# Moving Pool's two-input work, summing a softmax on ScalarE, sharing k and v buffers, and a new way to choose the order of an attention and expert kernel

## The chip, the core and the metric

The kernel runs on one core of a Trainium2 chip. A core has a matrix engine (TensorE, PE in the profile), a vector engine (VectorE, DVE), an activation engine (ScalarE, ACT), a general engine (GpSimd, POOL) and a queue engine (SyncE, SP), each with its own in-order list of instructions, and DMA engines that move data between the large memory (HBM) and the on-chip memory (SBUF). Matrix results land in a small accumulator memory (PSUM). The engines wait for each other by semaphores. The metric is the device time of one execution, in microseconds (us); a lower number is better.

## What is computed

Attention with two parts, then a gated feed-forward layer, all in fp32 (`B, H, S, D = 8, 8, 576, 64`, 512 model columns, 1024 hidden columns):

```python
q_d = q.reshape(B, H, Sd, factor, D).mean(axis=3)      # factor 4, Sd 144; k_d, v_d alike
out_up = np.repeat(sm_attn(q_d, k_d, v_d), factor, axis=2)
mask = np.abs(pos[:, None] - pos[None, :]) < factor     # seven neighbours
scores = np.where(mask, scale * np.matmul(q, k.transpose(0, 1, 3, 2)), -1000000000.0)
out_local = np.matmul(softmax(scores), v)
x = (out_up + out_local).transpose(0, 2, 1, 3).reshape(B * S, H * D)
return ((x @ w1) * (x @ w2) @ w3) @ w_out
```

The weights arrive as 64-bit floats.

## The kernel before

**Units and chunks.** Each of the 8 batches is cut into 3 units of 12 positions for 16 blocks and 8 heads (192 rows of x). Two units make a chunk of 384 rows, so there are 24 units and 12 chunks. `moe(c)` takes chunk c through the feed-forward layer: for each of 8 slices `f` of the hidden columns, 24 matmuls into two `pab` tiles, ScalarE's copy `a` (L870), VectorE's product `a` (L872), and a split of it into a high and a low half, `gh` (ScalarE, L877) and `gl` (VectorE, L879); then 9 matmuls of `acc` with the folded weight `wphl` = w3 @ w_out. Three matmuls, high x high, high x low and low x high, stand for one fp32 product. `o_sb` (L887) takes the result out and SP stores it.

**The opening.** The 64-bit weights are loaded raw by SP and rebuilt to fp32 on chip: ScalarE's rebase (L285) and low word (L293, or Pool's L295), VectorE's L298 and L302. `fold` multiplies w3 by w_out on TensorE (`accw`, L337), and `gate_weights` splits w1 and w2 into a high half (ScalarE, L384) and a low half (Pool's subtraction, L386).

**Pooled attention, every batch.** `pair` works on two heads at a time: scores `s_ps`, a maximum on VectorE (L459), exponentials with sums on ScalarE (`pexp`, L468), a division by the sum on Pool (L477), transposes `t_ps` (L484), and, after four pairs, the products `o_ps` into `oup`.

**Local attention, two ways.** For the batches in `PB = (0, 1)`, `group_unit` does it on TensorE in groups of 16 pooled positions: `se_ps`, a mask, a softmax over `se` (VectorE's maximum L636, subtraction L637, ScalarE's exponential L638, VectorE's sum L639, division L642), transposes `te_ps`, products `oe_ps`. `pooled_sums` loads q and k for those batches and adds their four phases up, q on VectorE (L531), k on Pool (L549). For the other batches, `unit` does it on VectorE: seven products `pr` of q with shifted k (L727), their sums over 64 elements (VectorE's L740; for two of seven, ScalarE's L737), a small softmax `s_t`, seven products `pv` of v with it (VectorE's L794, for two of seven ScalarE's L786), and their addition into `xl`, by VectorE's L804 or by an accumulating DMA that Pool issues (L802, the numbers in `SHARE["dma_add"]`). Then a transpose `xt` (L808), the addition of `oup` (L815) and the split into `xh` and `xl` (L821, L822) for the chunk. The units can't start before the last group unit is through, since their tiles use the same memory.

**Buffers.** `BUFS` says how many of each tile there are: one `k_t` and two `v_t` in `unit`, so the k of a unit is loaded when the last `pr` of the unit before is done.

**What sets the order.** Every piece is a `Task` with an engine, an assumed cost, its predecessors and the buffers it takes. `Plan.run` lists the tasks on the engines by priority, forward and backward in turn, and `Plan.order` keeps the list with the earliest end of all rounds. The functions are then called in that order, which fixes each engine's queue.

## Time and profile before

| | |
|---|---|
| median of 3 runs | 816.15 us (813.66 to 818.69) |
| the profiled execution | 811.43 us, its span 809.6 us |
| TensorE busy | 763.1 us, 94% of the span |
| VectorE busy | 645.4 us, 80% |
| ScalarE busy | 525.1 us, 65% |
| Pool busy | 200.3 us, 25% |
| DMA | 118.98 MB, 147 GB/s on average |

The span runs from the first to the last recorded instruction of one execution. A row of the profile's groups has line, engine, operation, tiles, shapes and count, then the busy time and the mean of one in ns, then the idle time of that engine ahead of it and who ended it. A row of the waits has the total, the number and the longest. Busy times of single instructions overlap where an engine pipelines them.

### The profile page before, as it was taken

Reading aid. Unit: us, or ns where it says so; the run is one execution under the profiler, and the core shown is the slowest. Engines: PE = TensorE matmul, PEld = TensorE weight load, DVE = VectorE, ACT = ScalarE, POOL = GpSimd, SP = SyncE. Lnnn points to the kernel's source line nnn. Section 1 sums busy time; section 2 is a strip of 40 time slices with the busy share of each in tenths; the row PEclk is TensorE's granted clock in tenths of the full one; section 3 lists DMA queues with packets and bytes.
Section 4 is the critical chain, followed back from the end, with each engine's and each line's share of the span. In section 5 each row is a group of like instructions: output and inputs, shape, how many; then the busy total and the mean of one; then the engine's idle time right before and its main releaser. Section 6 shows DMA issues by size and latency. Waiting matters only on the chain.

```text
span 809.6 us, 15110 instructions
## 1 busy us (share of the span) xinstructions
PE 763.1 (94%) x5256; PEld 657.2 (81%) x5256; DVE 645.4 (80%) x1121; ACT 525.1 (65%) x2040; POOL 200.3 (25%) x211
## 2 busy tenths in 40 slices
PE   4899888999999999999999999999997999999995
PEld 1344467898999899998998999798997988999994
DVE  5889997967899998998999989799886898853111
ACT  4676656445877878867877697587783788742211
POOL 5321666300221323321312221222221221110000
PEclk9999999999999999999999999999998999999998
DMA  8975654813389759947858659855576853351101
GB/s 289 303 243 186 192 138 148 163 43 128 108 196 213 152 125 221 191 116 182 179 128 216 146 101 225 182 119 126 137 169 154 185 116 81 72 104 20 40 1 39
DMA packets 44067, 118.98 MB, mean 147 GB/s; under 512 B 5320, under 2 KB 11464, under 8 KB 43992
## 3 DMA queue, kind: packets, MB, share of 16 engines
q0 software_dynamic: 15264, 46.02, 32.5%
q1 hardware_dynamic: 28728, 72.01, 27.4%
q8 instruction: 41, 0.67, 0.3%
q14 instruction: 34, 0.28, 0.1%
HBM read 80.26 MB, written 9.44 MB: 111 GB/s over the span
## 4 chain that ended last, share of the span: by engine, by line
PE 59%; DVE 15%; DMA 14%; ACT 6%; issue 4%; POOL 0%; SPq 0%; DVEq 0%; ACTq 0%; POOLq 0%
PE pab L253 12%; PE pab L255 11%; PE pab L254 11%; PE acc L253 6%; PE acc L255 6%; PE acc L254 6%; DMA k_t<-in_kw_dram 4%; DMA xl<-pv 4%; DMA out_dram<-o_sb 3%; DVE pr L727 2%; DMA raw<-in_w_dram 2%; PE s_ps L456 2%; DVE wx L302 1%; ACT pexp L468 1%; DMA raw<-in_wout_dram 1%
## 5 line engine op out<-in xcount | busy, mean ns | idle before, releaser
L786 ACT ACTIVATE pv<-v_t,s_t 128x64 f32<-128x64 f32 x432 | 114.1, 343 | 28.3 <-DMA xl<-pv 16.1
L727 DVE TENSOR_TENSOR pr<-q_t,k_t 128x768 f32<-128x768 f32 x126 | 117.5, 951 | 15.7 <-DMA k_t<-in_kw_dram 15.7
L802 POOL DMA_DIRECT2D xl<-pv x72 | 65.2, 906 | 261.4 <-DVE xl L804 130.2
L737 ACT ACTIVATE junk<-pr 128x64 f32<-128x64 f32 x432 | 111.2, 257 | 19.7 <-DVE pr L727 9.5
L253 PE MATMUL acc<-wphl,gh 128*128 128x512 f32 x288 | 116.3, 404 | 1.7 <-ACT o_sb L887 1.7
L255 PE MATMUL acc<-wphl,gl 128*128 128x512 f32 x288 | 113.6, 395 | 1.8 <-DVE gl L879 1.8
L254 PE MATMUL acc<-wphl,gh 128*128 128x512 f32 x288 | 113.0, 392 | 0.0
L872 DVE TENSOR_TENSOR a<-pab,a 128x384 f32<-128x384 f32 x96 | 53.0, 552 | 55.4 <-PE pab L255 50.1
L870 ACT COPY a<-pab 128x384 f32<-128x384 f32 x96 | 45.7, 476 | 69.7 <-PE pab L255 55.2
L879 DVE TENSOR_TENSOR gl<-a,gh 128x384 fp32r<-128x384 f32 x96 | 55.7, 580 | 36.6 <-ACT gh L877 36.1
L740 DVE TENSOR_REDUCE s_t<-pr 128x12 f32<-128x768 f32 x90 | 84.0, 943 | 0.1
L737 ACT ACTIVATION_READ_ACCUMULATOR junk<-pr 128x1 f32 x432 | 81.7, 189 | 0.0
L877 ACT CAST gh<-a 128x384 fp32r<-128x384 f32 x96 | 49.0, 510 | 49.1 <-PE acc L254 39.5
L337 PE MATMUL accw<-wo,w 128*128 128x512 f32 x128 | 65.6, 646 | 15.7 <-DVE w L302 13.6
L477 POOL TENSOR_TENSOR pexp<-pexp,grs 72x576 f32<-72x576 f32 x32 | 50.4, 1576 | 111.1 <-DVE grs L476 63.5
L253 PE MATMUL pab<-xh,w2b 128*128 128x384 f32 x192 | 66.1, 344 | 5.0 <-DVE a L872 5.0
L794 DVE TENSOR_TENSOR pv<-v_t,s_t 128x768 f32<-128x768 f32 x72 | 70.5, 979 | 0.1
L253 PE MATMUL pab<-xh,w1b 128*128 128x384 f32 x192 | 66.4, 346 | 1.4 <-ACT a L870 1.4
L253 PE MATMUL pab<-xh,w1a 128*128 128x384 f32 x192 | 66.4, 346 | 0.5 <-DVE wphl L357 0.5
L253 PE MATMUL pab<-xh,w2a 128*128 128x384 f32 x192 | 66.2, 345 | 0.7 <-ACT a L870 0.7
L255 PEld LDWEIGHTS acc<-wphl,gl 128*128 128x128 f32 x288 | 54.2, 188 | 14.5 <-DVE gl L879 2.3
L255 PE MATMUL pab<-xh,w2b 128*128 128x384 f32 x192 | 65.4, 340 | 0.0
(109 smaller groups left out, 1832.2 us busy)
## 6 DMA issues: line engine op xcount, KB each, us to landing
xl<-pv POOLq DMA_DIRECT2D x72, 384.0 KB, 5.1
raw<-in_w_dram SPq DMA_DIRECT2D x32, 512.0 KB
qks<-in_qk_dram POOLq DMA_DIRECT2D x18, 576.0 KB, 7.9
k_t<-in_kw_dram SPq DMA_DIRECT2D x18, 576.0 KB
v_t<-in_vw_dram SPq DMA_DIRECT2D x18, 576.0 KB
out_dram<-o_sb SPq DMA_DIRECT2D x33, 256.0 KB
vs<-in_v_dram POOLq DMA_DIRECT2D x24, 288.0 KB, 5.8
q_t<-in_q_dram SPq DMA_DIRECT2D x18, 384.0 KB
```

Of the source, the lines that this page charges most:

```text
L253: nc.tensor.matmul(out_ps, lhsT=lh, rhs=rh, start=first, stop=False)
L254: nc.tensor.matmul(out_ps, lhsT=lh, rhs=rl, start=False, stop=False)
L255: nc.tensor.matmul(out_ps, lhsT=ll, rhs=rh, start=False, stop=last)
L337: nc.tensor.matmul(accs[m], lhsT=T["x"][:, j % 4 * 128:j % 4 * 128 + 128], rhs=wo[0][:, j], start=j == 0, stop=j == NF - 1)
L727: (nc.gpsimd if o in share["qk_pool"] else nc.vector).tensor_tensor(out=T[o], in0=T["q"], in1=T["k"][:, o * D:o * D + nq].rearrange("p (t ...
L737: nc.scalar.activation(out=junk, in_=T[o][:, t], func=AF.Copy, accum_out=T["s"][:, t, o:o + 1])
L740: reds.append(add("DVE", dve_us(nq), lambda o=o: nc.vector.tensor_reduce(out=T["s"][:, :, o], in_=T[o], op=ALU.add, axis=AX.X), [tp], uses ...
L786: nc.scalar.mul(out=T["pv", o][:, tt], in_=T["v"][:, (tt + o) * D:(tt + o + 1) * D], mul=T["s"][:, tt, o:o + 1])
L794: nc.vector.tensor_tensor(out=T["pv", o], in0=T["v"][:, o * D:o * D + nq].rearrange("p (t d) -> p t d", d=D), in1=T["s"][:, :, o].unsqueez ...
L802: t = add("Pool", 1.04, lambda o=o: nc.gpsimd.dma_start(out=T["x"], in_=T["pv", o], accum_op=ALU.add), [t, tm], uses=[hx, h], late=dma_us( ...
L872: tg = add("DVE", dve_us(CT), lambda f=f: nc.vector.tensor_tensor(out=T["a", f], in0=T["p", 1, f], in1=T["a", f], op=ALU.mult), [ta, ends[ ...
L879: tl = add("DVE", dve_us(CT), lambda f=f: nc.vector.tensor_tensor(out=T["gl", f], in0=T["a", f], in1=T["gh", f].bitcast(F32), op=ALU.subtr ...
```

## The change

Five things change.

1. Pool gives up its two-input operations in the opening. The low halves of the gate weights and the k sums of batches 0 and 1 are computed on VectorE; the division in `pair`, for batches 0 and 1, by four ScalarE scalings. Pool keeps the division of the other batches, its share of the weight words, and the DMA issues.
2. The softmax of `group_scores` becomes six ScalarE exponentials per tile, each with the negative maximum as bias and a sum of its own. VectorE's subtraction and sum go, a small multiplication of the maximum comes.
3. In `unit`, k and v take turns in three buffers named `kv`. One of the four additions by DMA (number 5) goes to VectorE.
4. The transposes of the two heads of a pair (and of a quad) are one task that takes two PSUM banks.
5. The planner tries three assumptions on the speed of DMA (`SLOW`), replays each list with randomly longer durations, and keeps the one with the lowest mean. The output is stored in pieces that end at unit borders.

```diff
-BUFS = dict(..., q=2, k=1, v=2, ...)
+BUFS = dict(..., q=2, kv=3, ...)
-SHARE = dict(qk_pool=(), qk_act=(2, 4), av_act=(3, 5), dma_add=(2, 4, 5, 6))
+SHARE = dict(qk_pool=(), qk_act=(2, 4), av_act=(3, 5), dma_add=(2, 4, 6))
...
+SLOW = [(slow, 0.18) for slow in (1.0, 1.1, 1.2)]
+VARY = 0.03
+RARE = 0.01
+SEEDS = 4
+ROUNDS = 8
...
+    def replay(self, order, seed):
+        rng, tasks = random.Random(seed), self.tasks
+        end, free, dma = [0.0] * len(tasks), {}, 0.0
+        for i in order:
+            t = tasks[i]
+            x = free.get(t.eng, 0.0)
+            for j in self.pre[i]:
+                x = max(x, end[j] + (0.0 if tasks[j].eng == t.eng == "PE" else LATENCY))
+            x += t.cost if t.eng in ("PE", "SP") else t.cost * (1 + abs(rng.gauss(0, VARY))) + (rng.random() < RARE)
...
+        for slow, spare in SLOW:
+            now = self.run([-x for x in far], 0.05, slow=slow, spare=spare)
+            for _ in range(ROUNDS):
+                back = self.run([-x for x in now[2]], 0.05, back=True, slow=slow, spare=spare)
+                tried = [self.run([-x for x in back[2]], z, slow=slow, spare=spare) for z in SLACKS]
...
+        self.best = min(found, key=lambda f: f[:2])[2]
...
-                tl = add("Pool", pool_us(nw), lambda T=T: nc.gpsimd.tensor_tensor(out=T["p"][:, 1], in0=T["x"], in1=T["p"][:, 0].bitcast(F32), op=ALU.subtract), [th], uses=[wx])
+                tl = add("DVE", dve_us(nw), lambda T=T: nc.vector.tensor_tensor(out=T["p"][:, 1], in0=T["x"], in1=T["p"][:, 0].bitcast(F32), op=ALU.subtract), [th], uses=[wx])
...
+        if b in PB:
+            no = []
+            for par in range(2):
+                for qb in range(2):
+                    no.append(add("ACT", act_us(SD, 1), lambda par=par, qb=qb: nc.scalar.mul(out=T["p"][:, par, qb], in_=T["p"][:, par, qb], mul=T["rs"][:, par, qb:qb + 1]), [rs], uses=[hg, hp]))
...
-            fl, bank = add("PE", 4 * 0.062, flip, [no], take=[R["ps"]], uses=[hp])
+        fl, *banks = add("PE", 8 * 0.062 + SWITCH / 2, flip, no, take=[R["ps"], R["ps"]], uses=[hp])
...
-                    nc.gpsimd.tensor_tensor(out=to, in0=x[:, 0] if f == 1 else to, in1=x[:, f], op=ALU.add)
-                t = add("Pool", pool_us(2 * SD), total, [t, first], uses=[hk4, hq])
+                    nc.vector.tensor_tensor(out=to, in0=x[:, 0] if f == 1 else to, in1=x[:, f], op=ALU.add)
+                t = add("DVE", dve_us(2 * SD), total, [t, first], uses=[hk4, hq])
...
-        t = add("DVE", dve_us(n2), lambda: nc.vector.tensor_tensor(out=p3(), in0=p3(), in1=wide_(U["mx"]), op=ALU.subtract), [t], uses=[hs])
-        t = add("ACT", act_us(n2), lambda: nc.scalar.activation(out=U["p"], in_=U["p"], func=AF.Exp, scale=1.0 / D ** 0.5), [t], uses=[hs])
-        t = add("DVE", dve_us(n2), lambda: nc.vector.tensor_reduce(out=U["sm"], in_=p3(), op=ALU.add, axis=AX.X), [t], uses=[hs])
+        t = add("DVE", 0.16, lambda: nc.vector.tensor_scalar_mul(U["mx"], U["mx"], -1.0 / D ** 0.5), [t], uses=[hs])
+        ex = []
+        for i in range(2 * NG):
+            ex.append(add("ACT", act_us(GK, 2), lambda i=i: nc.scalar.activation(out=p3()[:, i], in_=p3()[:, i], func=AF.Exp, bias=U["mx"][:, i:i + 1], scale=1.0 / D ** 0.5, accum_out=U["sm"][:, i:i + 1]), [t], uses=[hs]))
...
-            T["k"] = pools["dvp"].tile([128, nk], F32, name="k_t", bufs=BUFS["k"])
+            T["k"] = pools["dvp"].tile([128, nk], F32, name="kv", bufs=BUFS["kv"])
...
-            T["v"] = pools["dvp"].tile([128, nk], F32, name="v_t", bufs=BUFS["v"])
+            T["v"] = pools["dvp"].tile([128, nk], F32, name="kv", bufs=BUFS["kv"])
```

Pool's queue in the opening, before, from the last words of the folded weights to the k sums of batch 1 (`w1a` is the first half of the split w1, `wx` its rebuilt source, `qks` the pooled q and k):

```order
L295 TENSOR_SCALAR raw<-raw 128x512 x3
L386 TENSOR_TENSOR w1a<-wx,w1a 128x512 x2
L295 TENSOR_SCALAR raw<-raw 128x512
L386 TENSOR_TENSOR w1a<-wx,w1a 128x512 x2
L549 TENSOR_TENSOR qks<-k_828 128x288
L549 TENSOR_TENSOR qks<-k_866 128x288
L549 TENSOR_TENSOR qks<-qks,k_828 128x288
```

The same place in Pool's queue now:

```order
L323 TENSOR_SCALAR raw<-raw 128x512 x5
L439 DMA vs<-in_v_dram 72x1024 x2
L323 TENSOR_SCALAR raw<-raw 128x512 x2
L439 DMA vs<-in_v_dram 72x1024
L323 TENSOR_SCALAR raw<-raw 128x512 x3
```

Only weight words and DMA issues are left. The subtractions stand in VectorE's queue now, between the group softmax of batch 0 (`se`, `emx`) and the rebuilding of further weights (`raw`, `wx`):

```order
L330 SCALAR_TENSOR_TENSOR wx<-wx,raw 128x512
L711 TENSOR_TENSOR xl_836<-xf,xh_835 128x2x192
L662 TENSOR_TENSOR se<-se_ps,band 128x216
L702 TENSOR_TENSOR xf<-oe_ps,oup 128x192 x2
L671 TENSOR_REDUCE emx<-se 128x6
L672 TENSOR_SCALAR emx<-emx 128x6
L414 TENSOR_TENSOR w1a<-wx,w1a 128x512
L326 SCALAR_TENSOR_TENSOR raw<-raw 128x512
L414 TENSOR_TENSOR w1a<-wx,w1a 128x512
```

ScalarE's queue at the first group softmax (`se`), before, with the rebuilding of weights (`raw`, `w`, `wx`) around it:

```order
L293 ACTIVATE raw<-raw 128x512
L638 ACTIVATE se<-se 128x432
L293 ACTIVATE raw<-raw 128x512
L285 ACTIVATE wx<-raw 128x512
L285 ACTIVATE w_641<-raw 128x512
L638 ACTIVATE se<-se 128x432
L293 ACTIVATE raw<-raw 128x512
```

And now:

```order
L321 ACTIVATE raw<-raw 128x512
L675 ACTIVATE se,esm<-se,emx 128x72 x12
L313 ACTIVATE w_691<-raw 128x512
L321 ACTIVATE raw<-raw 128x512
L313 ACTIVATE w_705<-raw 128x512
L629 COPY pte<-te_ps 72x3x2x64 x2
L384 CAST wphl<-accw 128x512 x2
```

Twelve exponentials stand in one row ahead of the next weight, where one stood, then three other pieces, then one.

VectorE's queue at the turn from one unit to the next, before. The row just ahead of these is the last product with the unit's k, which frees the one `k_t`; the last row here is the first product with the next k (`k_t_6218`):

```order
L740 TENSOR_REDUCE s_t_5982<-pr_6196 128x12
L740 TENSOR_REDUCE s_t_5982<-pr_6207 128x12
L872 TENSOR_TENSOR a_6228<-pab_6198,a_6228 128x384
L747 TENSOR_TENSOR s_t_5982<-s_t_5982,edge_sb_72 128x3x3
L752 TENSOR_REDUCE mx_6241<-s_t_5982 128x12
L754 TENSOR_TENSOR s_t_5982<-s_t_5982,mx_6241 128x84
L794 TENSOR_TENSOR pv_6251<-v_t_5576,s_t_5617 128x768
L759 TENSOR_REDUCE sm_6261<-s_t_5982 128x12
L761 TENSOR_SCALAR sm_6261<-sm_6261 128x12
L762 RECIPROCAL sm_6261<-sm_6261 128x12
L763 TENSOR_TENSOR s_t_5982<-s_t_5982,sm_6261 128x84
L727 TENSOR_TENSOR pr_6275<-q_t_5873,k_t_6218 128x768
```

Now, at the unit with the fewest rows between the two. The first row is the last product with the v of the unit before the last (`kv_7078`), which frees the buffer; the last row is the first product with the next k (`kv_7829`), which is loaded into it:

```order
L830 TENSOR_TENSOR pv_7814<-kv_7078,s_t_7164 128x768
L840 TENSOR_TENSOR xl_7461<-xl_7461,pv_7774 128x768
L915 TENSOR_TENSOR gl_7799<-a_7729,gh_7798 128x384
L487 TENSOR_REDUCE gmx_7831<-s_ps_7835 72x2
L487 TENSOR_REDUCE gmx_7831<-s_ps_7836 72x2
L488 TENSOR_SCALAR gnb_7832<-gmx_7831 72x4
L908 TENSOR_TENSOR a_7844<-pab_7786,a_7844 128x384
L830 TENSOR_TENSOR xl_7872<-kv_7421,s_t_7492 128x768
L830 TENSOR_TENSOR pv_7883<-kv_7421,s_t_7492 128x768
L503 TENSOR_SCALAR grs_7834<-gsm_7833 72x4
L504 RECIPROCAL grs_7834<-grs_7834 72x4
L763 TENSOR_TENSOR pr_7909<-q_t_7369,kv_7829 128x768
```

The load hangs on another row than before, and at this unit eleven rows lie between them. On SP, the load of k is now followed at once by the load of the same unit's v.

More of the change, by code (lines that the diff above doesn't have):

```diff
@@ L1 @@
+import random
 from contextlib import ExitStack
@@ L108, in link, with run @@
                 self.then[at[d]].append(i)
-    def run(self, prio, slack, back=False):
+    def run(self, prio, slack, back=False, slow=1.0, spare=LATENCY):
         tasks = self.tasks
@@ L152, in run @@
             for j in suc[i]:
-                can[j] = max(can[j], x + (0.0 if e == tasks[j].eng == "PE" else LATENCY))
+                can[j] = max(can[j], x + (LATENCY if "PE" not in (e, tasks[j].eng) else 0.0 if e == tasks[j].eng else spare))
                 left[j] -= 1
@@ L167, in run @@
         return max(end), start, end, order
+    def replay(self, order, seed):
[7 more added lines that the diff above has]
+            x += t.cost if t.eng in ("PE", "SP") else t.cost * (1 + abs(rng.gauss(0, VARY))) + (rng.random() < RARE)
+            free[t.eng] = x
+            if t.late:
+                dma = max(dma, x + 1.3) + t.late * (1.05 + abs(rng.gauss(0, 3 * VARY)))
+                x = dma + 0.8 + rng.random()
+            end[i] = x
+        return max(end)
     def order(self):
@@ L175, in order @@
             far[i] = self.tasks[i].cost + self.tasks[i].late + max([far[j] for j in self.suc[i]], default=0.0)
-        now = self.run([-x for x in far], 0.05)
-        best = now
-        for _ in range(ROUNDS):
-            back = self.run([-x for x in now[2]], 0.05, back=True)
-            now = min((self.run([-x for x in back[2]], z) for z in SLACKS), key=lambda r: r[0])
-            best = min(best, now, key=lambda r: r[0])
-        self.best = best
-        return [self.tasks[i] for i in best[3]]
+        found = []
+        self.log = []
+        for slow, spare in SLOW:
[3 more added lines that the diff above has]
+                tried = [self.run([-x for x in back[2]], z, slow=slow, spare=spare) for z in SLACKS]
+                now = min(tried, key=lambda r: r[0])
+                self.log.append((slow, spare, round(now[0], 1), round(min(sum(self.replay(r[3], k) for k in range(SEEDS)) / SEEDS for r in tried), 1)))
+                found += [(sum(self.replay(r[3], k) for k in range(SEEDS)) / SEEDS, len(found) + i, r) for i, r in enumerate(tried)]
+        self.best = min(found, key=lambda f: f[:2])[2]
+        self.mean = min(found)[0]
+        return [self.tasks[i] for i in self.best[3]]
 def dve_us(n, fast=False):
@@ L484, in flip @@
                         nc.tensor.transpose(out=T[par][:, kb, qb * QB:qb * QB + QB], in_=T["p"][:, par, qb, kb * QB:kb * QB + QB], identity=ident[:QB, :QB])
-            fl, bank = add("PE", 4 * 0.062, flip, [no], take=[R["ps"]], uses=[hp])
+        fl, *banks = add("PE", 8 * 0.062 + SWITCH / 2, flip, no, take=[R["ps"], R["ps"]], uses=[hp])
+        for par, bank in enumerate(banks):
             def keep(par=par):
@@ L582, in rest, with flip @@
             for qd, (U, hs, no) in enumerate(quads):
-                for par in range(2):
-                    def flip(par=par, U=U):
+                def flip(U=U):
+                    for par in range(2):
                         U["t", par] = ps.tile([GK, NG, 2 * GQ], F32, tag="g", name="te_ps", bufs=BUFS["ps"])
@@ L587, in flip @@
                             nc.tensor.transpose(out=U["t", par][:, g], in_=U["p"][:, par, g], identity=ident)
-                    fl, bank = add("PE", NG * 0.062, flip, [no], take=[R["ps"]], uses=[hs])
+                fl, *banks = add("PE", 2 * NG * 0.106, flip, no, take=[R["ps"], R["ps"]], uses=[hs])
+                pep.append(fl)
+                for par, bank in enumerate(banks):
                     def keep(par=par, U=U, qd=qd):
```

44 lines of the change are left out of this document (22 added, 22 removed).

## The prediction

> **What bounds the kernel now.** I read the page's totals first, then the busy time stage by stage, then TensorE's waits.
>
> ```profile
> span 809.6 us, 15110 instructions
> PE 763.1 (94%) x5256; PEld 657.2 (81%) x5256; DVE 645.4 (80%) x1121; ACT 525.1 (65%) x2040; POOL 200.3 (25%) x211
> ...
> 0.00:79.60 79.60, 61.97 (x454) 28.97 (x454) 63.88 (x125) 50.74 (x110) 27.52 (x43) 1.00 0.80 258
> 79.60:106.00 26.40, 21.37 (x176) 10.85 (x176) 25.29 (x52) 17.72 (x36) 15.30 (x14) 0.94 0.53 153
> 106.00:150.00 44.00, 39.26 (x435) 32.97 (x435) 37.78 (x69) 25.89 (x70) 28.81 (x26) 1.00 0.63 161
> 150.00:185.00 35.00, 35.00 (x531) 31.71 (x527) 25.48 (x66) 14.24 (x31) 2.57 (x3) 1.00 0.41 82
> 190.00:740.00 550.00, 540.07 (x3324) 492.42 (x3323) 480.44 (x787) 401.82 (x1762) 125.63 (x126) 0.99 0.65 148
> 740.00:800.00 60.00, 60.00 (x312) 55.82 (x312) 10.60 (x19) 11.71 (x24) 0.00 (x0) 1.00 0.05 14
> ```
>
> The window rows give stretch, length, then busy us of TensorE, weight load, VectorE, ScalarE and Pool, TensorE's clock, and the DMA share. TensorE is the bound: 763.1 of 809.6 us. Its idle time is the whole room: 17.6 us to 79.6, 5.0 to 106, 4.7 to 150, none to 185, 9.9 between 190 and 740 (550 - 540.07), none from there to 800, and the end. VectorE is close behind: 25.29 of 26.40 us around 90, and 480.44 of 550 in the middle.
>
> ```profile
> PE accw L337 <- DVE w L302: 13.6, 5, 9.0
> PE pab L253 <- DVE a L872: 5.0, 2, 4.5
> PE pab L253 <- ACT a L870: 2.0, 2, 1.4
> PE acc L255 <- DVE gl L879: 1.8, 1, 1.8
> ```
>
> These are TensorE's waits (total, times, longest). Of the first 17.6 us, 13.6 are waits for the first weights and come before anything the change touches. The gaps that it can reach early are 17.6 - 13.6 = 4.0, 5.0 and 4.7, so 13.7 us. In the middle, 4.5 and 1.8 us stand behind VectorE's `a` and `gl`. The chain and VectorE's own waits say why:
>
> ```profile
> DVE pr L727 <- DMA k_t<-in_kw_dram: 15.7, 6, 6.3
> DVE a L872 <- PE pab L255: 17.3, 17, 4.8
> ...
> 513.14 8.90 DMA k_t<-in_kw_dram
> 600.54 16.91 DMA k_t<-in_kw_dram
> ```
>
> `k_t` has one buffer, so its load is issued when the last product of the unit before is done, and VectorE then stands still for up to 6.3 us. The two TensorE gaps follow at once. An idle gap also slows what follows it:
>
> ```profile
> 96.00:100.00 4.00, 4.00 (x14) 0.57 0.54 151
> 444.00:448.00 4.00, 4.00 (x23) 1.00 0.73 115
> 524.00:528.00 4.00, 3.52 (x14) 0.78 0.80 139
> 528.00:532.00 4.00, 4.00 (x19) 0.79 0.65 118
> 620.00:624.00 4.00, 4.00 (x13) 0.50 0.09 33
> 624.00:628.00 4.00, 4.00 (x16) 0.84 0.93 144
> ```
>
> After TensorE, the fourth number is the granted clock. Behind the 4.5 us gap 2.0 + 0.6 us are lost to it, behind the 1.8 us gap 0.9 + 0.8, behind a gap near 95 another 1.7; behind the 1.4 us gap at 443, none. So the two k gaps cost 4.5 + 1.8 + 2.6 + 1.7 = 10.6 us together. The Trainium skill, "TensorE: Matmul & The Clock Gate", section "Why this matters for your kernels", would have the clock fall only for idle gaps above about 3 us. By that the k gaps cost 8.9 us; the 0.78 and 0.79 behind a gap of 1.8 us speak against it here, and the sum keeps 10.6.
>
> **The change part by part, first the opening batches.** Pool's 16 gate subtractions, 12 k sums and 8 of 32 normalizations go, and so does what they do to VectorE:
>
> ```profile
> 82.37 0.60 DVE L637 TENSOR_TENSOR se<-se,emx 128x432 f32<-128x432 f32 x1
> 82.89 0.68 DVE L302 SCALAR_TENSOR_TENSOR wx<-wx,raw 128x512 int32<-128x512 int32 x1
> 84.80 1.67 DVE L637 TENSOR_TENSOR se<-se,emx 128x432 f32<-128x432 f32 x1
> ...
> 83.19 2.81 POOL L386 TENSOR_TENSOR w1a<-wx,w1a 128x512 fp32r<-128x512 f32 x2 [1.28 <-ACT w1a L384]
> ...
> L298 DVE SCALAR_TENSOR_TENSOR raw<-raw 128x512 int32<-128x512 int32 x40 | 35.0, 882 | 8.6 <-ACT raw L293 8.5
> L302 DVE SCALAR_TENSOR_TENSOR wx<-wx,raw 128x512 int32<-128x512 int32 x16 | 16.2, 1018 | 0.5 <-ACT wx L285 0.2
> L637 DVE TENSOR_TENSOR se<-se,emx 128x432 f32<-128x432 f32 x12 | 9.4, 787 | 0.1
> L639 DVE TENSOR_REDUCE esm<-se 128x6 f32<-128x432 f32 x12 | 7.0, 590 | 0.4 <-ACT se L638 0.3
> L638 ACT ACTIVATE se<-se 128x432 f32<-128x432 f32 x12 | 6.8, 566 | 8.4 <-DVE se L637 8.4
> ```
>
> The same subtraction takes 0.60 us alone and 1.67 us beside Pool's. At 0.69 us undisturbed (0.68 in the row at 82.89), L298 loses 40 x 0.19 = 7.7 us and L302's `wx` 16 x 0.33 = 5.2, in all 12.9. VectorE also loses its own group subtraction and sum, 9.4 + 7.0 = 16.4. It gains 16 gate subtractions of 0.68 (10.9), 12 sums of 288 elements, taken at 0.45 between a third and the whole of L637's 0.60 (5.4), and 12 small multiplies (2.4 at 0.2). Net about -10.6 us on VectorE before 185; if Pool's remaining work keeps all of the slowing, +2.3.
>
> ScalarE gets the bill: 72 exponentials of 72 elements with a sum, and 32 scalings of 144.
>
> ```profile
> L737 ACT ACTIVATE junk<-pr 128x64 f32<-128x64 f32 x432 | 111.2, 257 | 19.7 <-DVE pr L727 9.5
> L737 ACT ACTIVATION_READ_ACCUMULATOR junk<-pr 128x1 f32 x432 | 81.7, 189 | 0.0
> ...
> 33.91 1.44 ACT pexp L468 x8
> ...
> 321.14 2.41 ACT pv L786 x10
> ```
>
> A summing activation is two instructions, 0.257 + 0.189 = 0.45 us if they don't overlap; four such pairs of `pexp` in 1.44 us are 0.36 each, so they do. At 0.40 the 72 cost 28.8 us. A scaling of 64 elements goes at 0.24 (2.41 / 10); 144 are put at 0.31, 9.9 us. Less L638's 6.8 that is 32 us more on ScalarE, whose busy time to 185 goes from 108.6 (50.74 + 17.72 + 25.89 + 14.24) to about 140. The Trainium skill, "Perfetto Trace Analysis", section "Optimizing Scalar/DVE Operations", speaks against cutting an operation up: about 93 ns for each extra ScalarE instruction. By that the 60 extra ones cost 5.6 us, not the 22 above, and the net would be 15.5; the accumulator rows say it is more.
>
> On TensorE's path the opening can give between -13.7 - 1.7 (all gaps and the clock behind them) and, if ScalarE fills up, about +16 (below). VectorE is the engine that is 96% busy there (25.29 of 26.40) and it is the one relieved, while ScalarE has 26.8 us free of 70.4 between 79.6 and 150; I take a third of the room: **-5 us**.
>
> **k and v share three buffers.** The k of a unit now needs the buffer of the v two units back, no longer that of the k just used. The orders say how much earlier that is. Between the row that frees the buffer and the first product, before has 10 to 29 VectorE rows, mean 15.8, over the last 16 units; now 11 to 24, mean 18.4. A row is worth 0.61 us (480.44 / 787), so a load of 8.9 us needs 14.6 rows. Before, seven units fall short, by 16.2 rows together (9.9 us; measured 15.7); now three, by 6.8. So the wait shrinks to 0.42 of itself and does not vanish: 58% of the 10.6 us of gaps, **-6 us**, with ends at -10.6 and 0, or at +4 where a v load, now queued right behind its k load on SP and waiting there for k's last product, keeps output stores behind it. v itself has 50 rows or more, so it is covered.
>
> **One add per unit moves from DMA to VectorE.**
>
> ```profile
> L804 DVE TENSOR_TENSOR xl<-xl,pv 128x768 f32<-128x768 f32 x36 | 35.5, 987 | 2.4 <-ACT pexp L468 1.0 <-DMA xl<-pv 0.9 <-ACT pv L786 0.5
> xl<-pv POOLq DMA_DIRECT2D x72, 384.0 KB, 5.1
> ...
> ACT pv L786 <- DMA xl<-pv: 16.1, 8, 3.4
> ```
>
> 18 x 0.987 = 17.8 us more on VectorE between 190 and 740; the k wait gives back 0.58 x 15.7 = 9.1, so 8.7 net on 550. The cover is VectorE's 17.3 us of waiting for TensorE (`pab`), which lies at the stage's end and is of less use in its middle; if none holds, +8.7 us. I charge a quarter, **+2**. In return each unit's sum has one DMA of 5.1 us less in its chain, and ScalarE's 16.1 us of waiting for `pv` buffers should lose a quarter; of the 1.4 us gap behind `a` L870 I credit half, **-0.7**.
>
> **The rest.** Eight transposes now go to TensorE in one piece where often two of four went, 18 fewer pieces (47 + 15 before, 32 + 12 now). From a piece's start to its end:
>
> ```profile
> 465.91 0.41 PE L484 MATMUL t_ps<-ident,pexp 72*72 72x72 f32 x4
> ...
> 487.19 0.67 PE L484 MATMUL t_ps<-ident,pexp 72*72 72x72 f32 x8
> ```
>
> Two pieces of four are 0.82 us against 0.67, so 18 x 0.15 = 2.7 us at most; the ends of a piece are pipelined into what follows it, and I take a third, **-0.8**. Nine more store issues on SP and shorter stores: nothing, beside TensorE's work; without that cover the loads behind them come later, as in the +4 above.
>
> Sum: -5 - 6 + 2 - 0.7 - 0.8 = -10.5 us. The profiled execution took 811.4 us, 1.8 above its span, so 801 on its scale. The three runs' median, 816.15, is 4.7 above it; that stays, since nothing read here says which stalls vary. 816.15 - 10.5 = 805.7, so **806 us**.
>
> **The rivals.**
> *Nearly all gaps go.* If VectorE's relief clears the opening (-15) and the k gaps vanish (-10.6): 816.15 - 15 - 10.6 + 2 - 1.5 = 791. For it: six waits for k carry most of the middle's gaps, and the unit's chain loses a DMA. Against it: the three short leads. Chance 0.20.
> *VectorE takes back what the buffers give.* The 8.7 us land on TensorE, since a static order can't use slack at the end; -5 - 6 + 8.7 - 1.5 = -4, 812. For it: 480.44 + 17.8 - 9.1 = 489 of 550 busy, with no DMA wait to blame. This includes the case that the shared buffers don't do what they say because the load still stands close to its use. Chance 0.20.
> *ScalarE bounds the opening: slower.* Between 79.6 and 150 ScalarE is busy 17.72 + 25.89 = 43.6 of 70.4 us; half of the 32 us falls there, 60 of 70. Its queue is in order, so a weight rebase, a transposed copy for TensorE and an `a` copy wait behind rows of exponentials. If its present waits for VectorE and TensorE (26.8 us idle) can't be filled, the stretch grows by the 16 us: 816.15 + 16 - 6 + 2 - 1.5 = 827. It decides once ScalarE's idle in that stretch is under some 6 us. The page's 93 ns would make it rarer. Chance 0.15.
> *The forecast.* Chance 0.45, between 798 and 811.
>
> **How the numbers follow.** A change within 1% (808.0 to 824.3) can't be told from none. Faster: the first rival and 0.33 of the forecast's 0.45, 0.53. Same: the other 0.12 and 0.17 of the second rival, 0.29. Slower: the third rival and 0.03 of the second, 0.18. The range goes from 788, just below the first rival, to 824: outside lie some 0.05 below and most of the third rival above.
>
> **What will show it.** Opening: VectorE's L298 and `wx` rows at 0.7 us; TensorE's waits for VectorE between 80 and 150 shrinking from most of 9.7 us of idle time; ScalarE's idle in that stretch above 6 us, no long waits of TensorE for `se` or `pexp`. Middle: VectorE's wait for the shared buffer's k load near 6.6 us (0.42 x 15.7), and at 524 and 620 no clock below 0.9. It is wrong if TensorE waits for `a` and `gl` more than the 6.8 us of now, if ScalarE shows no idle in the opening, or if TensorE's busy time itself moves by more than 3 us.

## The result and the profile after

The changed kernel takes **793.08 us** (median, 792.73 to 794.88), beside 815.21 for the kernel before on the same chip (813.66 to 818.69): **0.9727 of it, 95% interval 0.9691 to 0.9763**. The forecast of 806 had the direction, and the range held the time, but the gain is 22.1 us where 10.5 were forecast. The profiled execution took 792.73 us, its span 791.0.

The changed kernel's totals, and the same stages as before (TensorE, weight load, VectorE, ScalarE, Pool, TensorE's clock, DMA share, GB/s):

```profile
span 791.0 us, 15265 instructions
PE 760.2 (96%) x5256; PEld 653.7 (83%) x5256; DVE 645.0 (82%) x1155; ACT 552.1 (70%) x2204; POOL 139.3 (18%) x157
...
0.00:79.60 79.60, 65.81 (x481) 30.80 (x482) 61.35 (x145) 61.11 (x170) 12.95 (x31) 1.00 0.81 253
79.60:106.00 26.40, 22.36 (x175) 13.38 (x174) 24.86 (x58) 23.09 (x57) 3.62 (x4) 0.94 0.76 223
106.00:150.00 44.00, 44.00 (x530) 38.61 (x533) 35.46 (x81) 36.08 (x132) 11.07 (x15) 1.00 0.74 170
150.00:185.00 35.00, 35.00 (x469) 31.78 (x459) 20.16 (x50) 16.76 (x61) 0.00 (x0) 1.00 0.34 103
190.00:740.00 550.00, 546.74 (x3377) 496.65 (x3377) 491.47 (x805) 401.94 (x1748) 111.65 (x108) 1.00 0.58 133
```

VectorE is as busy as before (645.0 us against 645.4) and TensorE nearly so (760.2 against 763.1). What went is TensorE's idle time: from 17.6 to 13.8 us in the first stage, 5.0 to 4.0 and 4.7 to 0 in the next two, and 9.9 to 3.3 in the middle. These stages give 16.1 us. Over the whole span TensorE's idle time fell by 15.7 us (46.5 to 30.8) and its busy time by 2.9, with the same number of matmuls and a mean granted clock of 0.994 in place of 0.987; together that is the 18.6 us by which the span shrank.

The waits of the changed kernel (engine, tile and line, what it waited for; total, times, longest), the last four rows from 180 to 750 us alone:

```profile
PE accw L365 <- DVE w L330: 12.1, 6, 9.2
...
POOL xl L838 <- DVE xl L840: 220.5, 41, 17.0
DVE pr L763 <- DMA kv<-in_kw_dram: 5.1, 3, 3.4
ACT pv L822 <- DMA xl<-pv: 7.4, 3, 3.7
PE pab L281 <- DVE a L908: 1.9, 2, 1.7
```

VectorE still waits for k, three times, 5.1 us (15.7 before). One of these waits makes the largest gap that TensorE has left in the middle, 1.7 us at 642. Pool's 220.5 us are the time in which its next DMA addition stands behind VectorE's addition of the same sum.

The groups of instructions that the opening part was reckoned from, in the changed kernel (busy us, mean ns of one, idle time before them):

```profile
L326 DVE SCALAR_TENSOR_TENSOR raw<-raw 128x512 int32<-128x512 int32 x40 | 27.6, 694 | 10.4 <-ACT raw L321 8.1 <-POOL raw L323 1.9
L330 DVE SCALAR_TENSOR_TENSOR wx<-wx,raw 128x512 int32<-128x512 int32 x16 | 11.3, 712 | 1.2 <-ACT wx L313 0.5
L675 ACT ACTIVATE se<-se,emx 128x72 f32<-128x72 f32 x72 | 24.7, 349 | 0.8 <-DVE emx L672 0.8
L675 ACT ACTIVATION_READ_ACCUMULATOR se<-se,emx 128x1 f32 x72 | 13.9, 193 | 0.0
L509 ACT ACTIVATE pexp<-pexp,grs 72x144 f32<-72x144 f32 x32 | 10.6, 407 | 0.7 <-DVE grs L504 0.6
```

The two rebuilding steps go at 0.694 and 0.712 us in place of 0.882 and 1.018.

### The profile page after: what moved, and what is told of

It reads as the page before. It is cut to its first block, busy times and chain, and to the rows that moved or that the text cites. A ratio compares the mean times of both kernels' runs of the same rounds, so it can differ in the third digit from the quotient of the medians.

```text
span 791.0 us, 15265 instructions
## 1 busy us (share of the span) xinstructions
PE 760.2 (96%) x5256; PEld 653.7 (83%) x5256; DVE 645.0 (82%) x1155; ACT 552.1 (70%) x2204; POOL 139.3 (18%) x157
## 4 chain that ended last, share of the span: by engine, by line
PE 83%; DMA 6%; DVE 5%; ACT 3%; SPq 1%; issue 1%; POOL 1%; ACTq 0%; DVEq 0%; POOLq 0%
PE pab L281 17%; PE pab L283 16%; PE pab L282 16%; PE acc L281 8%; PE acc L283 8%; PE acc L282 8%; DMA raw<-in_w_dram 3%; PE s_ps L484 2%; PE o_ps L453 2%; PE t_ps L519 2%; PE accw L365 1%; DMA kv<-in_kw_dram 1%; PE oe_ps L693 1%; POOL pexp L511 1%; PE te_ps L622 1%
## 5 line engine op out<-in xcount | busy, mean ns | idle before, releaser
L822 ACT ACTIVATE pv<-kv,s_t 128x64 f32<-128x64 f32 x432 | 114.7, 340 | 20.1 <-DVE s_t L799 12.8
L763 DVE TENSOR_TENSOR pr<-q_t,kv 128x768 f32<-128x768 f32 x126 | 117.4, 950 | 8.0 <-DMA kv<-in_kw_dram 5.1
L838 POOL DMA_DIRECT2D xl<-pv x54 | 47.5, 881 | 268.9 <-DVE xl L840 220.5
L281 PE MATMUL pab<-xh,w1a 128*128 128x384 f32 x192 | 66.3, 345 | 2.7 <-DVE wphl L385 2.7
L830 DVE TENSOR_TENSOR pv<-kv,s_t 128x768 f32<-128x768 f32 x72 | 68.6, 962 | 0.2
L281 PE MATMUL pab<-xh,w2b 128*128 128x384 f32 x192 | 65.9, 343 | 1.9 <-DVE a L908 1.9
L281 PE MATMUL pab<-xh,w2a 128*128 128x384 f32 x192 | 65.9, 343 | 0.0
L283 PE MATMUL pab<-xh,w1a 128*128 128x384 f32 x192 | 65.4, 340 | 0.0
L282 PE MATMUL pab<-xl,w1a 128*128 128x384 f32 x192 | 65.2, 340 | 0.0
L283 PE MATMUL pab<-xh,w2a 128*128 128x384 f32 x192 | 64.8, 337 | 0.0
```

Source lines behind the costliest of these rows:

```text
L281: nc.tensor.matmul(out_ps, lhsT=lh, rhs=rh, start=first, stop=False)
L282: nc.tensor.matmul(out_ps, lhsT=lh, rhs=rl, start=False, stop=False)
L283: nc.tensor.matmul(out_ps, lhsT=ll, rhs=rh, start=False, stop=last)
L763: (nc.gpsimd if o in share["qk_pool"] else nc.vector).tensor_tensor(out=T[o], in0=T["q"], in1=T["k"][:, o * D:o * D + nq].rearrange("p (t ...
L822: nc.scalar.mul(out=T["pv", o][:, tt], in_=T["v"][:, (tt + o) * D:(tt + o + 1) * D], mul=T["s"][:, tt, o:o + 1])
L830: nc.vector.tensor_tensor(out=T["pv", o], in0=T["v"][:, o * D:o * D + nq].rearrange("p (t d) -> p t d", d=D), in1=T["s"][:, :, o].unsqueez ...
```

## The experiments

The change has four parts that can be made one by one, here called *opening* (Pool's subtractions, sums and normalizations, and the group softmax), *addition 5* (DMA to VectorE), *buffers* (k and v share three) and *choice* (the planner's way to choose an order). The merged transposes and the shorter stores were not undone or tried by themselves: the kernels with one part undone keep them, those with one part alone and `oa` have the old ones. The theory after the result was that one of them, or luck among the orders, gives the 11 us that the sum lacks. The rival: the parts are not independent, and each is worth little until the others are there.

### One part undone

`u_open`, with a new plan; the same for the 12 k sums, the normalizations and the group softmax, all as in the kernel before:

```diff
-                tl = add("DVE", dve_us(nw), lambda T=T: nc.vector.tensor_tensor(out=T["p"][:, 1], ...
+                tl = add("Pool", pool_us(nw), lambda T=T: nc.gpsimd.tensor_tensor(out=T["p"][:, 1], ...
```

> The changed kernel with the opening's work where it was: gate subtractions, k sums and all divisions on Pool, the group softmax in one exponential with VectorE's subtraction and sum; planned anew. Theory of the moved work: TensorE's idle time before 150 us goes from 17.8 back to 25 to 28 us, 801 to 805 us. Rival, the choice of order: 793 to 797 us with the idle time still near 18.

`u_add`, with a new plan:

```diff
-SHARE = dict(qk_pool=(), qk_act=(2, 4), av_act=(3, 5), dma_add=(2, 4, 6))
+SHARE = dict(qk_pool=(), qk_act=(2, 4), av_act=(3, 5), dma_add=(2, 4, 5, 6))
```

> The changed kernel with the fourth addition by DMA again. By the prediction's terms (+2 for VectorE's extra add, -0.7 for the chain) this should be 1 us faster, 791 to 793 us. If the shorter chain of DMAs is worth more than VectorE's 17 us, it is slower: 795 to 800 us, with TensorE waits behind a and more of ScalarE's waiting for pv buffers than 7.4 us.

`u_kv`, with a new plan:

```diff
-            T["k"] = pools["dvp"].tile([128, nk], F32, name="kv", bufs=BUFS["kv"])
+            T["k"] = pools["dvp"].tile([128, nk], F32, name="k_t", bufs=BUFS["k"])
...
-            T["v"] = pools["dvp"].tile([128, nk], F32, name="kv", bufs=BUFS["kv"])
+            T["v"] = pools["dvp"].tile([128, nk], F32, name="v_t", bufs=BUFS["v"])
```

> The changed kernel with separate buffers again, one for k and two for v, planned anew. Theory of the moved work: VectorE's wait for k comes back to 13 to 16 us from 5.1, TensorE's gaps behind a and gl return with the lower clock after them, 799 to 803 us. Rival, the choice of order: the planner puts other work into the wait, at most 3 us lost, 793 to 796 us.

`u_plan`:

```diff
-        for slow, spare in SLOW:
...
-        self.best = min(found, key=lambda f: f[:2])[2]
+        now = self.run([-x for x in far], 0.05)
+        best = now
+        for _ in range(ROUNDS):
+            back = self.run([-x for x in now[2]], 0.05, back=True)
+            now = min((self.run([-x for x in back[2]], z) for z in SLACKS), key=lambda r: r[0])
+            best = min(best, now, key=lambda r: r[0])
+        self.best = best
```

> The changed kernel with the old way of choosing the order (one DMA speed, 16 rounds, the earliest end, no replays). Theory of the moved work: the gain comes from the work taken off VectorE's path and from the shared buffers, so this stays within 3 us of the changed kernel, 793 to 796 us. Rival, the choice of order: the replays made the gain, and with it the runs' nearness to each other; then 800 us or more, with runs that lie 3 to 5 us apart as before.

Measured, as ratios to the kernel before: without the opening 813.14 us, 0.9974 [0.994, 1.0007]; without addition 5 815.4, 0.9987 [0.9961, 1.0012]; without the buffers 804.31, 0.9852 [0.9808, 0.9897]; without the choice 803.26, 0.9854 [0.9801, 0.9907]. Undoing them costs 20, 22, 11 and 10 us, 64 in all, of a gain of 22. So no single part gives it. Without the opening or without addition 5 nothing measurable is left. Both came out above every range written down for them. `u_plan` came out as the rival of the order said. `u_kv` took a little more than the 799 to 803 of the moved-work theory, but not by its mechanism: with the old buffers VectorE waits for k even less than the 5.1 us of the changed kernel, as its waits from 180 to 750 us show:

```profile
DVE pr L763 <- DMA k_t<-in_kw_dram: 2.5, 1, 2.5
```

### One part alone

`o_open`, `o_add`, `o_kv` and `o_plan` are the kernel before with one part each, planned anew. The edits are those above the other way round, so of each only a line:

```diff
+            ex.append(add("ACT", act_us(GK, 2), lambda i=i: nc.scalar.activation(out=p3()[:, i], in_=p3()[:, i], func=AF.Exp, bias=U["mx"][:, i:i + 1], ...
```

> The kernel before with the opening's part alone (gate subtractions and k sums on VectorE, divisions of two batches and the group softmax on ScalarE), planned in the old way. If the parts add up, it gives the opening's idle time, 8 to 11 us: 805 to 808 us. Rival, all limits have to go together: TensorE gets to the middle earlier and waits there for VectorE's units, under 5 us: 811 to 816 us.

```diff
+SHARE = dict(qk_pool=(), qk_act=(2, 4), av_act=(3, 5), dma_add=(2, 4, 6))
```

> The kernel before with addition 5 of each unit on VectorE and nothing else changed, planned in the old way. Theory of the DMA chain: three additions by DMA in a row held the units' buffers and Pool's queue, and this was most of the loss; alone it gives 10 to 18 us, 798 to 806 us. Rival, all limits have to go together: with the opening's Pool work, one k buffer and the old order it gives under 5 us, 811 to 816 us. By the prediction's term (+2 - 0.7) it gives nothing, 816 us.

```diff
+BUFS = dict(pr=3, pv=3, xl=2, xt=1, q=2, kv=3, w3=5, ...
```

> The kernel before with k and v in three shared buffers and nothing else changed. If the parts add up, VectorE's wait for k falls from 15.7 to 4 to 8 us and 5 to 10 us are gained, 806 to 811 us. Rival, all limits have to go together: the wait goes to the additions by DMA, 812 to 816 us.

```diff
+        for slow, spare in SLOW:
+            now = self.run([-x for x in far], 0.05, slow=slow, spare=spare)
```

> The kernel before with the new way of choosing the order and nothing else. With the changed kernel's work the old way cost 10 us. If the way of choosing is worth this by itself, 804 to 808 us, with runs nearer to each other than 7 us; if it only pays once the work leaves it room, 812 to 816 us.

Measured: the opening alone 809.81 us, 0.9913 [0.9886, 0.994]; addition 5 alone 817.16, 1.0042 [1.0001, 1.0082]; the buffers alone 819.02, 1.0036 [0.9999, 1.0073]; the choice alone 815.55, 0.9999 [0.9967, 1.0032]. The four add up to -0.1%; together they give -2.7%. The opening's time lies between its two ranges, the other three lie in those of the rival or up to 3 us above: the parts are not independent. One limit of these comparisons: all of them but `o_plan` are planned in the old way, each as one list, and how far two lists of that planner lie apart was not measured.

Waits of the kernel with the opening alone, from 180 to 750 us:

```profile
POOL xl L809 <- DMA xl<-pv: 108.9, 24, 9.5
ACT pv L793 <- DMA xl<-pv: 12.7, 7, 3.9
DVE pv L801 <- DMA xl<-pv: 11.0, 4, 4.6
PE pab L253 <- ACT a L877: 6.5, 5, 2.7
DVE pr L734 <- DMA k_t<-in_kw_dram: 2.8, 3, 1.7
```

The wait for k, on which the prediction put the middle's gaps, has all but gone here (2.8 us of 15.7), with one k buffer. Yet TensorE's idle time from 190 to 740 stays at 10.4 us: VectorE now waits for `pv` buffers that the DMA additions hold (11.0 us), ScalarE still does (12.7 us, 16.1 before), and TensorE waits for ScalarE's `a`. With the buffers alone the k wait stays, in the same view of that kernel:

```profile
DVE pr L727 <- DMA kv<-in_kw_dram: 13.5, 5, 5.8
```

### The opening and addition 5 together

`oa`, the kernel before with these two parts and no others:

```diff
+SHARE = dict(qk_pool=(), qk_act=(2, 4), av_act=(3, 5), dma_add=(2, 4, 6))
...
+            ex.append(add("ACT", act_us(GK, 2), lambda i=i: nc.scalar.activation(out=p3()[:, i], in_=p3()[:, i], func=AF.Exp, bias=U["mx"][:, i:i + 1], ...
```

> The kernel before with two parts of the change, the opening work and addition 5 on VectorE, without the shared buffers and with the old way of choosing the order. If the parts add up as they did alone (-5.8 and +1.5), 811 us. If these two are enough and the other two parts are worth nothing beside them, 793 to 797. With either of the other two parts as well it took 803 to 804, so if each of those still gives something, 804 to 811.

Measured: 799.74 us, **0.9813 [0.9776, 0.9851]**. Alone the two are worth -0.9% and +0.4%; together -1.9%, two thirds of the whole gain. The time lies between the ranges that were expected.

Two runs from above belong beside it. `u_plan` is this kernel with the shared buffers, the merged transposes and the shorter stores; `u_kv` is it with the new choice, the transposes and the stores. Both took longer than it (803.26 and 804.31 us). So beside these two parts neither the buffers nor the choice gave anything by itself, and only with both of them there it became 6.7 us less. Differences of 4 to 5 us between kernels that are planned anew may also be the order alone.

Windows from 0 to 190 and from 190 to 740 us, columns as above. First the opening stage of the kernel before:

```profile
0.00:190.00 190.00, 162.60 (x1622) 108.91 (x1623) 154.32 (x315) 110.55 (x253) 74.67 (x86) 0.99 0.65 189
```

Of the kernel with the opening alone:

```profile
0.00:190.00 190.00, 167.43 (x1624) 112.60 (x1625) 137.07 (x332) 136.96 (x418) 29.47 (x50) 0.96 0.63 185
190.00:740.00 550.00, 539.62 (x3330) 490.17 (x3329) 470.31 (x786) 396.83 (x1761) 126.41 (x126) 1.00 0.65 150
```

Of the kernel with addition 5 alone:

```profile
0.00:190.00 190.00, 162.84 (x1599) 107.63 (x1600) 154.04 (x309) 108.84 (x244) 71.62 (x85) 0.96 0.62 182
190.00:740.00 550.00, 540.66 (x3334) 490.25 (x3333) 491.08 (x807) 407.29 (x1770) 130.87 (x108) 1.00 0.58 138
```

Of the kernel with both:

```profile
0.00:190.00 190.00, 168.34 (x1636) 114.46 (x1637) 136.70 (x328) 136.18 (x411) 29.36 (x49) 0.97 0.62 182
190.00:740.00 550.00, 545.29 (x3375) 498.80 (x3374) 490.69 (x812) 400.98 (x1773) 113.84 (x108) 1.00 0.59 138
```

TensorE's idle time to 190 us was 27.4 in the kernel before; it is 22.6 with the opening, 27.2 with addition 5, 21.7 with both: the opening's 5 us come either way. In the middle it was 9.9, and is 10.4, 9.3 and 4.7: there neither does anything without the other. In the changed kernel it is 17.8 and 3.3. With addition 5 alone, other waits had taken the place of the k wait, as its waits from 180 to 750 us show:

```profile
PE t_ps L484 <- POOL pexp L477: 6.5, 5, 3.6
DVE pr L727 <- DMA k_t<-in_kw_dram: 0.7, 1, 0.7
DVE xl L804 <- DMA xl<-pv: 8.7, 4, 3.6
```

### Addition 5 in the changed kernel's own order

The planner makes a new order for every edit. The next three runs keep the changed kernel's order and change only what is issued at one place of it. `f_add` issues addition 5 as a DMA:

```diff
-... lambda o=o: nc.vector.tensor_tensor(out=T["x"], in0=T["x"], in1=T["pv", o], op=ALU.add), [t, tm], uses=[hx, h])
+... lambda o=o, i=i: nc.gpsimd.dma_start(out=T["x"], in_=T["pv", o], accum_op=ALU.add) if i == 5 else nc.vector.tensor_tensor(...), [t, tm], uses=[hx, h])
```

> The changed kernel's own order, word for word, with one thing put back: addition 5 of each unit goes by DMA at the place where VectorE's addition stands. With it planned anew the kernel took 815 us. If the DMA in the chain is the cause (three DMAs of 4.5 us one after another, where now VectorE's 0.96 us stands between two), this is slow as well: 803 to 815 us, with TensorE waits behind a and gl, ScalarE waiting for pv buffers and VectorE for xl. If the other order was the cause, it stays at 793 to 797 us: VectorE has 17 us less to do.

`f_copy` leaves addition 5 on VectorE and lets Pool issue a transfer of the same size that nothing waits for but the buffer:

```diff
+                        if i == 5:
+                            nc.gpsimd.dma_start(out=spare[n], in_=T["pv", o].rearrange("p t d -> p (t d)"))
                         nc.vector.tensor_tensor(out=T["x"], in0=T["x"], in1=T["pv", o], op=ALU.add)
```

> The changed kernel in its own order, addition 5 on VectorE as it is there, and at the same place Pool also issues a DMA of the same 384 KB that carries the same pv buffer to a spare array in DRAM. This leaves the sum's chain as it is, but holds the pv buffer for a transfer and puts one more transfer per unit on Pool's queue and the 16 DMA engines. If addition 5 as a DMA cost 30 us because of the buffers or the traffic, this comes out near it, 812 to 823 us. If it cost that because a third transfer of some 5 us stood in the chain of each sum, with Pool and VectorE waiting for it in order, this stays at 793 to 798.

`f_none` leaves addition 5 out:

```diff
+                        if i != 5:
+                            nc.vector.tensor_tensor(out=T["x"], in0=T["x"], in1=T["pv", o], op=ALU.add)
-                    ... nc.vector.tensor_tensor(out=T["x"], in0=T["x"], in1=T["pv", o], op=ALU.add) ...
```

> The changed kernel in its own order with addition 5 left out altogether: neither VectorE nor a DMA makes it, so one of the seven products is missing from each sum. If VectorE's 18 x 0.99 = 17.8 us for it are covered by its waits for TensorE, the time stays within 2 us of the changed kernel's 793.1. If VectorE bounds the middle stage, up to 4 us (TensorE's 3.3 us of gaps there and their clock) go.

Measured: as a DMA 823.42 us, 1.0089 [1.0063, 1.0116]; with the copy 800.13, 0.9817 [0.9772, 0.9863]; left out 798.03, 0.9791 [0.9736, 0.9846]. The DMA in the chain costs 30 us over the changed kernel, more than was expected and more than the whole gain; the same bytes beside the chain cost 7, just above the 793 to 798 of the chain theory and far from the 812 to 823 of its rival. If the two simply add, up to 7 us are the transfer, its issue and the longer hold on the buffer, and some 23 come from having it in the chain. Waits with addition 5 as a DMA, from 180 to 750 us:

```profile
POOL xl L838 <- DVE xl L840: 119.7, 27, 15.0
POOL xl L838 <- DMA xl<-pv: 65.3, 10, 8.6
ACT pv L822 <- DMA xl<-pv: 28.9, 8, 7.1
DVE pv L830 <- DMA xl<-pv: 21.2, 10, 4.9
POOL xl L840 <- DMA xl<-pv: 18.7, 4, 6.0
...
PE pab L281 <- DVE a L908: 5.3, 4, 3.4
PE t_ps L519 <- POOL pexp L511: 4.9, 4, 1.8
PE acc L283 <- DVE gl L915: 4.4, 3, 3.3
PE pab L281 <- ACT a L906: 3.7, 3, 2.9
```

The transfers of all four DMA additions in that kernel (KB each, median us from issue to landing):

```profile
xl<-pv POOLq DMA_DIRECT2D x72, 384.0 KB, 4.2
```

The copy's, in the kernel with the copy:

```profile
spare_dram<-pv POOLq DMA_DIRECT2D x18, 384.0 KB, 5.6
```

A transfer takes no longer than the copy; but in the chain each starts only when the addition before it is done. TensorE's idle time in the middle grows from 3.3 to 19.9 us, and its busy time from 760.2 to 771.3, with the same matmuls at a mean granted clock of 0.984 in place of 0.994. The middle of this kernel, columns as above:

```profile
190.00:740.00 550.00, 530.12 (x3239) 476.27 (x3238) 471.33 (x777) 396.60 (x1745) 125.61 (x124) 0.99 0.64 144
```

The rows of waits say by which way. ScalarE and VectorE stand 50 us behind `pv` buffers that DMA additions still hold (28.9 + 21.2; in the changed kernel 7.4 and nothing), and TensorE's waits for their `a` and `gl` grow from 1.9 to 13.4 us (5.3 + 4.4 + 3.7). Pool stands 84 us behind the transfers (65.3 + 18.7), but it waits for its additions no longer in all than in the changed kernel, where 220.5 us stood behind VectorE's; TensorE's wait for Pool's `pexp` grows from 1.3 to 4.9 us only. So most of the new gaps lie behind VectorE and ScalarE, which the held buffers stop, and Pool's queue shows as the smaller part; no run separates the two. The largest gap but one shows it step by step (start, length, engine, line, operation, tiles, shapes, and the idle time before with what ended it):

```profile
516.65 0.96 DVE L830 TENSOR_TENSOR pv<-kv,s_t 128x768 f32<-128x768 f32 x1 [4.94 <-DMA xl<-pv]
...
520.99 0.55 DVE L915 TENSOR_TENSOR gl<-a,gh 128x384 fp32r<-128x384 f32 x1
...
521.60 0.80 PE L283 MATMUL acc<-wphl,gl 128*128 128x512 f32 x1 [3.29 <-DVE gl L915]
```

VectorE waits 4.94 us for a buffer, works off what stands in its queue, and reaches `gl` when TensorE has stood for 3.29 us.

Leaving the addition out gains nothing, so VectorE's 18 additions are covered. But neither range for it held: it loses 4.9 us. In its trace the wait for k grows from 5.1 to 8.9 us and the gap behind it from 1.70 to 3.50 us, probably since VectorE, without these 0.95 us, comes to its k earlier. The middle's 1.8 us more of idle time, the opening's 1.1 us and TensorE's 2.1 us more of busy time make 5.0 us; the spans differ by 4.7 (795.7 against 791.0). So a small shift in an order can cost as much as a part gains. The wait in the kernel without the addition:

```profile
DVE pr L763 <- DMA kv<-in_kw_dram: 8.9, 3, 5.2
```

### Pool's work in the changed kernel's own order

`f_pool` lets Pool do the 16 subtractions and 12 sums at VectorE's places in the order:

```diff
-... nc.vector.tensor_tensor(out=T["p"][:, 1], in0=T["x"], in1=T["p"][:, 0].bitcast(F32), op=ALU.subtract), ...
+... nc.gpsimd.tensor_tensor(out=T["p"][:, 1], in0=T["x"], in1=T["p"][:, 0].bitcast(F32), op=ALU.subtract), ...
...
-                    nc.vector.tensor_tensor(out=to, in0=x[:, 0] if f == 1 else to, in1=x[:, f], op=ALU.add)
+                    nc.gpsimd.tensor_tensor(out=to, in0=x[:, 0] if f == 1 else to, in1=x[:, f], op=ALU.add)
```

> The changed kernel's own order with the 16 gate subtractions and the 12 k sums issued to Pool instead of VectorE at the same places (the divisions and the group softmax stay as changed). Theory of the slowing: VectorE's rows with two inputs go from 0.69 and 0.71 us back to 0.8 to 1.0, TensorE's idle time before 150 us rises from 17.8 to 22 to 26, 797 to 802 us. Rival, Pool's help is free: VectorE has 15 us less to do and the time stays at 791 to 795.

Measured: 797.8 us, 0.979 [0.9742, 0.9838], 4.7 above the changed kernel and in the range of the slowing. The profiled run, at 802.2, is the longest of its four, so its stages show more than those 4.7 us. TensorE's idle time to 190 us is 22.1 in place of 17.8, later nearly the same, and its busy time is 4.8 us longer. In the groups of this kernel VectorE's rebuilding steps are slower again, by a fifth and by less than a third of the difference to the kernel before; 0.8 to 1.0 us was expected:

```profile
L326 DVE SCALAR_TENSOR_TENSOR raw<-raw 128x512 int32<-128x512 int32 x40 | 29.1, 731 | 13.8 <-ACT raw L321 9.6 <-POOL raw L323 3.9
L330 DVE SCALAR_TENSOR_TENSOR wx<-wx,raw 128x512 int32<-128x512 int32 x16 | 12.7, 801 | 1.3 <-ACT wx L313 0.3
```

So Pool's subtractions and sums cost some 5 us where they stand in this order, of the 20 that `u_open` lost with a new order. What the divisions and the group softmax cost, and what the new order, was not separated.

### Luck among the orders, and one step further

`seeds` replays the lists with other random numbers, `rank6` takes the seventh of the planner's ranking:

```diff
-... sum(self.replay(r[3], k) for k in range(SEEDS)) / SEEDS ...
+... sum(self.replay(r[3], k) for k in range(100, 100 + SEEDS)) / SEEDS ...
```

> The changed kernel with other random numbers in the replays, so that another of the tried lists is kept; 303 rows of VectorE's order differ. If the gain is in the work moved, any good list gives it: 791 to 796 us. If single orders matter by more than that, it lies 4 to 10 us off, and every comparison of kernels that are planned anew has to be read with that width.

```diff
-        self.best = min(found, key=lambda f: f[:2])[2]
+        self.best = sorted(found, key=lambda f: f[:2])[6][2]
```

> The changed kernel with the list that comes seventh in the replays instead of the first. If the ranking by replays means little, it is as good as the first: 791 to 796 us. If the ranking is what made the gain, it is 4 to 12 us slower, 797 to 805 us.

Measured: 793.16 us, 0.9735 [0.9686, 0.9783], and 793.6, 0.9728 [0.9685, 0.977]. Both orders differ from the changed kernel's in hundreds of VectorE's places and take the same time, so the changed kernel's gain is no lucky draw among the lists of the new planner.

`b_two` puts addition 6 on VectorE as well:

```diff
-SHARE = dict(qk_pool=(), qk_act=(2, 4), av_act=(3, 5), dma_add=(2, 4, 6))
+SHARE = dict(qk_pool=(), qk_act=(2, 4), av_act=(3, 5), dma_add=(2, 4))
```

> The changed kernel with addition 6 on VectorE as well, so that two of the six additions are DMAs, planned anew. If the chain of DMAs still holds the units, 788 to 792. If VectorE, with 491 + 18 of 550 us, now bounds them, 796 to 805. If neither, 793.

Measured: 797.48 us, 0.9784 [0.9736, 0.9832], no better than the changed kernel. That is in the range named for a middle that VectorE bounds, but the trace does not show it: VectorE is busy 508.7 of the middle's 550 us, TensorE idle 4.5, and only 0.6 us of that behind VectorE's `a`. Three DMA additions and three on VectorE are as good as any split tried. No run beat the changed kernel.

## Why the prediction was right and wrong

**Opening, -5.** Right in size for the part alone, and in mechanism as far as it was tested: TensorE's idle time to 190 us fell by 4.8, the time by 0.9% (4.9 to 9.3 us). The rebuilding steps came out at 0.694 and 0.712 us where 0.69 was taken. VectorE's busy time to 185 us fell by 10.6 us, as forecast (to the tenth by luck, as the stage's edge cuts other work), and ScalarE's rose to 137.0 (about 140 forecast). The pairs of summing exponentials took less than the 0.40 us assumed: in the chain of waits of the changed kernel six pairs, twelve records, follow each other in 2.15 us, 0.36 each.

```profile
60.72 2.15 ACT se L675 x12
```

The scalings of 144 are recorded with 0.407 us each, but their records overlap:

```profile
29.12 1.32 ACT L509 ACTIVATE pexp<-pexp,grs 72x144 f32<-72x144 f32 x4
```

With 0.407 for the last, the other three take (1.32 - 0.407) / 3 = 0.30 us each, as the 0.31 assumed. ScalarE kept 11.2 us of idle time between 79.6 and 150 (70.4 - 23.09 - 36.08), above the 6 at which it was to decide, so the rival that ends slower fell. That all of VectorE's slowing came from Pool's subtractions and sums is not shown: with these back on Pool in the changed order a fifth to three tenths of it returned. Inside the whole change the stage gave more, 9.6 us of TensorE's idle time (27.4 to 17.8).

**Shared buffers, -6.** The wait for k was forecast at 6.6 us and came out at 5.1, in three waits as counted; the middle lost 6.6 us of idle time. This looked like a hit and was not the cause: the wait goes equally with the old buffers (2.5 us in `u_kv`, 0.7 with addition 5 alone), and with the shared buffers alone it stays (13.5). The step that failed here is reading a wait's share of the gaps as the price of removing its cause. Where the k wait went, other waits held the same gaps (those behind the DMA additions in one run, for Pool's `pexp` in another). The prediction asked what is late next only for VectorE's own 8.7 us.

**Addition 5, +2 - 0.7.** Alone it measures +0.4%, about 3 us slower, where the two terms said 1.3. Beside the rest its absence costs 22 us, and in an unchanged order 30. **This is the step at which the size was lost: "each unit's sum has one DMA of 5.1 us less in its chain" was priced by ScalarE's 16.1 us of waiting, a quarter of it, and credited with half of one 1.4 us gap.** That wait was in the profile. Pool's behind the same transfers, from 180 to 750 us of the kernel before, was not read:

```profile
POOL xl L802 <- DMA xl<-pv: 25.6, 8, 6.2
```

What the DMA in the chain costs was seen only with it put back: 50 us of waiting for `pv` buffers and 16.6 us more of idle time on TensorE. The rows of waits show which limit is hit first in one order. They do not show the one just behind it.

**The sum.** The deeper failure: "-5 - 6 + 2 - 0.7 - 0.8" takes the parts as independent. Measured one by one they make -0.1%, together -2.7%. None of the signs of being wrong that the prediction names showed up. The rival "nearly all gaps go", 791, came nearest to the time, but that is partly luck: it took 15 us from the opening and 10.6 from the k gaps, where 9.6 and 6.6 us of idle time went and 2.9 us of busy time; the offset below makes up most of the rest. It was read as each part succeeding better, and not as the parts needing each other. "VectorE takes back what the buffers give" fell: with addition 5 left out the time doesn't drop.

**The offset.** On the profiled executions the sum was -10.5 and came out at -18.7 (811.4 to 792.7). The remaining 4.3 us of the miss are the offset: the median of the kernel before stands 4.7 above its profiled run, with runs spread over some 5 us, while the changed kernel's lies 0.35 above, with runs within 2.2 us. "That stays" was wrong. The gaps that are gone were probably those that varied; this was not tested by itself.

**Clock and merged transposes.** TensorE's busy time fell by 2.9 us, just inside the 3 allowed. At 524 and 620 no gap and no fall of the clock is left. What the merged transposes alone give was not measured.

What stays open is why a relieved opening helps the middle stage only when addition 5 is off the DMA. Every one of those kernels has another order from end to end, and nothing run here holds the order fixed for both; that part of it is luck among single orders of the old planner is not excluded.

## What to carry to other kernels

When a profile shows several engines nearly full and short waits of many kinds, the parts of a change need not be terms of a sum: removing one limit can let the next one hold the same gap, so a part can be worth nothing alone and twenty microseconds as the last one. Measure such a change from both ends, one part alone and one part undone, and keep the order fixed in some of the runs. And price a link in a dependent chain by everyone who stands behind it, first of all by those who wait for the buffers that it holds; here 18 DMA additions of 4.2 us each cost about 23 us in all by their place in the chain.
